# Compact retention output, a lag of three blocks and a new load order in a fused retention and feed-forward kernel

## The chip, the cores and the metric

The kernel runs on one core of one Trainium2 chip. The metric is device time in microseconds (us) of one execution. The kernel before was run again beside every experiment on the same chip. It took 249.6 to 253.2 us in all of these runs, mostly in two clusters near 249.8 and 252.5. The granted clock of PE was 1.00 over the runs of the lower one and 0.99 over those of the upper one; what starts the difference was not looked into. A ratio below is the mean time of one kernel's fast runs over the mean of the other's fast runs of the same rounds, so it is not quite the ratio of the medians quoted beside it.

Engine names in the profile: PE is the matmul engine (PEld its weight loads), DVE the vector engine, ACT the scalar engine, POOL the GpSimd engine, SPq the queue that issues most transfers. In the traces below each engine keeps the program order of its own instructions: PE stood for 6.05 us before one pair of score matmuls of the changed kernel while the matmuls behind them waited too.

## The reference

Retention for 4 batch rows, 8 heads, 768 steps and head size 64, followed by a feed-forward layer with 512 inputs and 2048 hidden units.

```python
def _attn_ref(q, k, v):
    gamma = 1.0 - 2.0 ** (-5.0 - np.arange(H))
    for t in range(S):
        state = gamma * state + einsum('bhd,bhe->bhde', k[:, :, t], v[:, :, t])
        y[:, :, t] = scale * einsum('bhd,bhde->bhe', q[:, :, t], state)

def _moe_ref(x, w_in, w_out):      # x: the 3072 tokens of y, heads side by side
    h = x @ w_in
    g = h * tanh(softplus(h))
    return g @ w_out
```

## The kernel before

The sequence is cut into 12 groups of 256 steps (two chunks of 128; three groups to a batch row). Heads go in pairs, so a group has four *units*. A unit has three steps:

```python
    def step_t(u):                       # T: transposes, then copies from PSUM
        ...
        for c in range(CG): nc.tensor.transpose(tp[:, 1, c], k16[:, c, hs(hp)], ident)
        for c in range(CG): nc.tensor.transpose(tp[:, 0, c], q16[:, c, hs(hp)], ident)
        nc.vector.tensor_copy(kt, tp[:, 1])
        nc.vector.tensor_copy(qp[0:64, :, 0], tp[0:64, 0])      # "pads": each head's q,
        nc.vector.tensor_copy(qp[64:128, :, 1], tp[64:128, 0])  # zeros for the other head

    def step_s(u):                       # S: scores, mask, state update
        for c in range(CG):
            nc.tensor.matmul(s_ps[:, c], kt[:, c], qp[:, c], start=True, stop=True)
        nc.vector.tensor_tensor(am, s_ps, msk[...], op=ALU.mult)
        ... # u_ps = k^T v per chunk; state = decay * state + u_ps, 128x128, on DVE

    def step_y(u):                       # Y: output, 256 columns = 2 heads x 128
        for c in range(CG):
            nc.tensor.matmul(y_ps[:, c], v16[:, c, hs(hp)], am[:, c], start=True, ...)
            if st is not None:
                nc.tensor.matmul(y_ps[:, c], st, qp[:, c], start=False, stop=True)
        for hh in range(2): nc.scalar.copy(xt[o:o + 64, ...], y_ps[o:o + 64, :, hh])
```

Half of what Y computes is thrown away: all 128 rows (two heads of v) meet all 256 columns (two heads of scores).

The retention steps are dealt out between the slices of the feed-forward layer. `f1` is one slice of the first matmul (8 matmuls of 256 columns), `f2` one of the second (4 of 512). Each block of 256 tokens has 8 slices, and f2 runs two blocks behind f1:

```python
    def att_ticks(u0, u1):
        for kk in range(u0, u1 + 2):
            yield lambda kk=kk: (step_y(kk - 2) ..., step_t(kk) ...)
            yield lambda kk=kk: (step_s(kk - 1) ...)
    ...
    for i in range(NG + 2):
        if i + 2 < NG: cast(i + 2)              # fp32 -> fp16, on GpSimd
        if i == 0:
            for j in range(NW): cast_wout(j)    # on GpSimd
        if 1 <= i and i + 3 < NG: load(i + 3)
        for a in range(NSL):
            ... # ticks up to i * NSL + a + 4
            if i < NG: f1(i, a)
            if 0 <= i - 2: f2(i - 2, a)
```

So a unit's T comes three ticks ahead of its S, and whole f1 slices lie in between. The loads are issued in the order group 0, four quarters of w_in, groups 1 and 2, four quarters of w_out, group 3, and so on.

## Time and profile before

| | before |
|---|---|
| median of its first 3 runs | 249.84 us |
| span of the profiled run | 250.4 us |
| PE busy | 220.4 us, 88% |
| first feed-forward matmul | 32.33 us |

The page of the kernel before, first part (busy us, share of the span, instructions) and second part (40 slices of the span, busy tenths; PEclk is the granted clock in tenths):

```profile
PE 220.4 (88%) x1696; PEld 157.5 (63%) x1696; DVE 116.5 (47%) x309; ACT 95.3 (38%) x195; POOL 85.1 (34%) x45
PE   0263199949999999999999999999999999999993
POOL 3102997679940450460640822703600000000000
DMA  8999999999912914916808609519210111011122
```

A slice is 6.26 us. PE is full from the sixth slice on, apart from one dip at 51 to 55 us. DMA is full for eleven slices: until about 67.5 us the kernel takes in data as fast as it can. From the dip on the kernel is bound by PE. The waits view of PE, the longest (line waited, releaser, us in total, times, longest):

```profile
PE tp L157 <- DVE k_142 L121: 9.2, 1, 9.2
PE tp L157 <- POOL k_277 L121: 7.8, 1, 7.8
PE tp L157 <- POOL k_504 L121: 3.7, 1, 3.7
```

These three waits are for the casts of groups 0, 1 and 3, and all three follow loads. In the timeline of PE, where idle time before a line would stand in brackets at its end, an early unit looks like this:

```profile
37.57 0.28 PE L157 MATMUL tp<-idtri,k_277 128*128 128x128 f16 x2
37.80 1.04 PE L228 MATMUL h_ps<-xt,win_87 128*128 128x256 f16 x8
38.67 0.38 PE L174 MATMUL s_ps<-qpad_90,kt 128*128 128x256 f16 x2
...
41.41 0.38 PE L174 MATMUL s_ps<-qpad_91,kt 128*128 128x256 f16 x2
```

The T at 37.57 has its S only at 41.41. Copies and pads have almost 4 us, and in these lines PE does not wait for them. One unit takes 2.74 us (38.67 to 41.41), and PE is full in it. Eight 256-column matmuls start 0.87 us apart in all.

### The profile page before, as it was taken

To read this page: it belongs to the slowest core of one execution; us is meant where nothing else is said; L and a number is where in the kernel's file an instruction comes from. 1 tells how busy PE (TensorE), PEld (TensorE's weight loads), DVE (VectorE), ACT (ScalarE), POOL (GpSimd) and SP (SyncE) were. 2 spreads that over 40 slices of the span, in tenths; PEclk is the share of its full clock that TensorE was granted. 3 is DMA by queue.
4 is the path that set the end of the run, shared out by engine and by line. 5 is a ranking of instruction groups with operands and counts; after the bars stand their busy time and mean duration, and the time that the engine had idled before them with its cause. 6 is when DMAs were issued, how large, how long until landed. Compare 5 with 4: busy or idle time off the path is not lost.

```text
span 250.4 us, 4251 instructions
## 1 busy us (share of the span) xinstructions
PE 220.4 (88%) x1696; PEld 157.5 (63%) x1696; DVE 116.5 (47%) x309; ACT 95.3 (38%) x195; POOL 85.1 (34%) x45
## 2 busy tenths in 40 slices
PE   0263199949999999999999999999999999999993
PEld 0141178827777777777777777777777777766441
DVE  1478567624455454535545553444655444101221
ACT  0324037624434445344444434444443444533000
POOL 3102997679940450460640822703600000000000
PEclk9999999998999999999999999999999999999999
DMA  8999999999912914916808609519210111011122
GB/s 162 297 387 263 218 287 387 256 207 227 181 42 66 225 46 106 195 40 149 190 0 176 162 3 229 106 46 228 66 42 0 45 45 41 3 42 45 44 81 84
DMA packets 82868, 33.91 MB, mean 135 GB/s; under 512 B 75552, under 2 KB 75680, under 8 KB 82848
## 3 DMA queue, kind: packets, MB, share of 16 engines
q1 hardware_dynamic: 82560, 33.56, 56.9%
q8 instruction: 13, 0.21, 0.4%
q10 hardware_dynamic: 288, 0.08, 0.1%
q14 instruction: 7, 0.06, 0.1%
HBM read 27.34 MB, written 6.29 MB: 134 GB/s over the span
## 4 chain that ended last, share of the span: by engine, by line
PE 77%; SPq 9%; DMA 7%; POOL 4%; issue 2%; DVE 0%; POOLq 0%
PE o_ps L241 33%; PE h_ps L228 29%; SPq L103 8%; DMA raw_q<-in_q_dram 4%; PE s_ps L174 3%; PE y_ps L205 3%; PE y_ps L209 3%; DMA raw_k<-in_k_dram 2%; PE tp L157 2%; PE tp L159 2%; PE u_ps L182 1%; SPq L130 1%; POOL q_276 L119 1%; POOL k_277 L121 1%; POOL k_504 L121 1%
## 5 line engine op out<-in xcount | busy, mean ns | idle before, releaser
L228 PE MATMUL h_ps<-xt,win_87 128*128 128x256 f16 x768 | 101.9, 277 | 0.0
L241 PE MATMUL o_ps<-wout_88,gt 128*128 128x512 f16 x384 | 95.9, 379 | 0.0
L232 ACT ACTIVATE gt<-h_ps 128x512 f16<-128x512 f32 x96 | 57.3, 597 | 96.0 <-PE h_ps L228 95.7
L228 PEld LDWEIGHTS <-win_87 128*128 128x128 f16 x768 | 72.7, 99 | 9.6
L241 PEld LDWEIGHTS <-gt 128*128 128x128 f16 x384 | 37.6, 98 | 28.2
L212 ACT CAST xt<-y_ps 64x256 f16<-64x256 f32 x96 | 35.1, 365 | 31.1 <-PE y_ps L209 30.5
L176 DVE TENSOR_TENSOR am<-s_ps,msk 128x512 f16<-128x512 f32 x48 | 33.0, 687 | 26.9 <-PE s_ps L174 26.8
L162 DVE COPY kt<-tp 128x256 f16<-128x256 f16 x48 | 14.0, 291 | 52.3 <-PE tp L159 52.3
L246 DVE COPY osb<-o_ps 128x512 f32<-128x512 f32 x24 | 16.6, 691 | 42.6 <-PE o_ps L241 42.6
L191 DVE SCALAR_TENSOR_TENSOR tstate<-tstate,tab,u_ps 128x128 f16<-128x128 f16 x64 | 21.9, 342 | 1.1
L174 PEld LDWEIGHTS <-kt 128*128 128x128 f16 x96 | 9.9, 105 | 8.7
L209 PEld LDWEIGHTS <-tstate 128*128 128x128 f16 x80 | 8.1, 101 | 4.1 <-DVE tstate L189 0.3
L157 PE MATMUL tp<-idtri,k_142 128*128 128x128 f16 x8 | 1.6, 308 | 10.1 <-DVE k_142 L121 9.2
L157 PE MATMUL tp<-idtri,k_277 128*128 128x128 f16 x8 | 1.3, 260 | 8.6 <-POOL k_277 L121 7.8
L142 POOL CAST wout_88<-wst 128x2048 f16<-128x2048 f32 x4 | 7.6, 1893 | 3.4 <-DMA wst<-in_moe_w_out_dram 3.2
L119 POOL TENSOR_TENSOR q_276<-raw_q,tab 128x1024 f16<-128x1024 f32 x1 | 2.8, 2777 | 16.1 <-DMA raw_q<-in_q_dram 16.1
L157 PEld LDWEIGHTS <-k_142 128*128 128x128 f16 x8 | 0.8, 126 | 10.6 <-DVE k_142 L121 9.2
L209 PE MATMUL y_ps<-qpad_91,tstate 128*128 128x256 f16 x28 | 7.4, 285 | 0.0
L209 PE MATMUL y_ps<-qpad_92,tstate 128*128 128x256 f16 x28 | 7.1, 278 | 0.0
L157 PEld LDWEIGHTS <-k_277 128*128 128x128 f16 x8 | 0.7, 110 | 9.5 <-POOL k_277 L121 8.2
L174 PE MATMUL s_ps<-qpad_91,kt 128*128 128x256 f16 x32 | 6.6, 291 | 0.0
L174 PE MATMUL s_ps<-qpad_92,kt 128*128 128x256 f16 x32 | 6.6, 291 | 0.0
(147 smaller groups left out, 226.9 us busy)
## 6 DMA issues: line engine op xcount, KB each, us to landing
raw_q<-in_q_dram SPq DMA_DIRECT2D x24, 256.0 KB, 5.0
raw_k<-in_k_dram SPq DMA_DIRECT2D x24, 256.0 KB, 5.1
raw_v<-in_v_dram SPq DMA_DIRECT2D x24, 256.0 KB, 5.0
out_dram<-osb SPq DMA_DIRECT2D x24, 256.0 KB, 2.0
wst<-in_moe_w_in_dram SPq DMA_DIRECT2D x4, 1024.0 KB, 9.2
wst<-in_moe_w_out_dram SPq DMA_DIRECT2D x4, 1024.0 KB, 10.4
idtri<-rn_identtri ACTq DMA_DIRECT2D x1, 64.0 KB, 3.1
tab<-rn_tab ACTq DMA_DIRECT2D x1, 10.0 KB, 1.9
```

The costliest lines, as they stand in the source:

```text
L103: nc.sync.dma_start(t[:, c], src[b, :, s0:s0 + C].rearrange("h p d -> p h d"))
L157: nc.tensor.transpose(tp[:, 1, c], k16[:, c, hs(hp)], ident)
L162: nc.vector.tensor_copy(kt, tp[:, 1])
L174: nc.tensor.matmul(s_ps[:, c], kt[:, c], qp[:, c], start=True, stop=True)
L176: nc.vector.tensor_tensor(am, s_ps, msk[:, hs(hp)].unsqueeze(1).broadcast_to((P, CG, 2, C)), op=ALU.mult)
L191: nc.vector.scalar_tensor_tensor(tn, states[-1], tab[:, 2 * H + hp:2 * H + hp + 1], u_ps[:, c], op0=ALU.mult, op1=ALU.add)
L209: nc.tensor.matmul(y_ps[:, c], st, qp[:, c], start=False, stop=True)
L212: nc.scalar.copy(xt[o:o + 64, hp, g * GT:(g + 1) * GT].rearrange("p (c i) -> p c i", i=C), y_ps[o:o + 64, :, hh])
L228: nc.tensor.matmul(h_ps[:, j], win16[:, bp, fb * P:(fb + 1) * P], xt[:, bp, i * GT:(i + 1) * GT], start=(bp == 0), stop=(bp == NBP - 1))
L232: nc.scalar.activation(gts[i][:, 2 * a:2 * a + 2], h_ps, AF.Mish, scale=inv_boost3)
L241: nc.tensor.matmul(o_ps, gts[i][:, fb, t * P:(t + 1) * P], wout16[:, fb], start=(fb == 0), stop=(fb == NFB - 1))
L246: nc.vector.tensor_copy(osb, o_ps)
```

## The change

The intent is to halve the wasted half of Y. The state matrix is kept block-diagonal, v is stored with a gap of zeros between the two heads, and both heads' outputs are accumulated into one 128-column tile. This takes 3 matmuls of 128 columns a chunk instead of 2 of 256, and one eviction instead of two. Along with it, feed-forward starts earlier through a new load order, f2 lags three blocks, and retention is put into fixed slots. The core of the diff (cut):

```diff
-        for c in range(CG):
-            nc.tensor.matmul(y_ps[:, c], v16[:, c, hs(hp)], am[:, c], ...)          # 256 columns
-            if st is not None:
-                nc.tensor.matmul(y_ps[:, c], st, qp[:, c], start=False, stop=True)  # 256 columns
+            if st is not None:
+                nc.tensor.matmul(y_ps[:, c], st, qt[:, c, hp], start=True, stop=False)   # 128
+            for hh in range(2):
+                nc.tensor.matmul(y_ps[:, c], vp[:, c * HP + hp, hh:hh + 2], am[:, c, hh], ...)  # 128
+        nc.scalar.copy(xts[g][:, hp], y_ps)
 ... state update
-            nc.vector.scalar_tensor_tensor(tn, states[-1], tab[...], u_ps[:, c], ...)  # 128x128
+            for hh in range(2):
+                o = slice(64 * hh, 64 * hh + 64)
+                nc.vector.scalar_tensor_tensor(tn[o, o], states[-1][o, o], ..., u_ps[o, c, o], ...)
 ... copies after the transposes
-        nc.vector.tensor_copy(qp[0:64, :, 0], tp[0:64, 0])
-        nc.vector.tensor_copy(qp[64:128, :, 1], tp[64:128, 0])
+        nc.vector.tensor_copy(qt[:, :, hp], tq[:, 0])
+        for hh in range(2):
+            nc.gpsimd.tensor_copy(qp[o:o + 64, :, hp, hh], qt[o:o + 64, :, hp])
 ... loads: group 0, w_in 0-1, group 1, w_in 2-3, groups 2 and 3, w_out
 ... schedule (slot = block * 8 + slice)
+    at(24, cast_wout, 0..3)                              # now on DVE
+    for g in range(4, NG):
+        s0 = max(20, (g - 1) * NSL - 12)
+        at(s0, cast, g, nc.gpsimd, nc.gpsimd, nc.gpsimd) # groups 4 and 5 both at slot 20
+    for g in range(1, NG):
+        for pos in range(-3, 7):                         # T at odd pos, S and Y at even pos
+            if g < 4: slot = (g - 1) * NSL + 4 + ((pos + 3) * 4) // 10   # half a block
+            else:     slot = (g - 1) * NSL + pos
+    for i in range(NG + LAG): ...                        # LAG = 3
```

The order of instructions shows two consequences. S now comes one slot after its T at most. In the first unit of groups 1 to 3 no matmul lies between the two. And GpSimd has the six casts of groups 4 and 5 ahead of the first pads of group 3.

More of the change, by code (lines that the diff above doesn't have):

```diff
@@ L42 @@
     FBW = NFB // NW
+    DT = 99
     BOOST = 16.0
-    inv_boost3 = float(1.0 / BOOST**3)
+    inv_boost = float(1.0 / BOOST**2)
     scale = float(1.0 / np.sqrt(D))
@@ L69 @@
     wst = ctx.enter_context(tc.tile_pool(name="rn_wst", bufs=4))
-    attp = ctx.enter_context(tc.tile_pool(name="rn_att", bufs=3))
-    stp = ctx.enter_context(tc.tile_pool(name="rn_state", bufs=3))
-    gtp = ctx.enter_context(tc.tile_pool(name="rn_gt", bufs=4))
-    outp = ctx.enter_context(tc.tile_pool(name="rn_out", bufs=3))
+    amp = ctx.enter_context(tc.tile_pool(name="rn_am", bufs=2))
+    xtp = ctx.enter_context(tc.tile_pool(name="rn_xt", bufs=3))
+    gtp = ctx.enter_context(tc.tile_pool(name="rn_gt", bufs=5))
+    outp = ctx.enter_context(tc.tile_pool(name="rn_out", bufs=2))
     psp = ctx.enter_context(
@@ L76 @@
     ctx.enter_context(tc.manual_schedule())
+    NPB = 3
     tab = cpool.tile([P, 2 * H + HP], FP32)
@@ L82 @@
     wout16 = cpool.tile([P, NFB, d_model], FP16)
-    xt = cpool.tile([P, HP, B * S], FP16)
-    NQP = 3
-    qpads = [
-        cpool.tile([P, CG, 2, C], FP16, name=f"qpad{i}") for i in range(NQP)]
+    qpads = [cpool.tile([P, CG, HP, 2, C], FP16, name=f"qpad{i}") for i in range(NPB)]
+    vpads = [cpool.tile([P, CG * HP, 3, D], FP16, name=f"vpad{i}") for i in range(NPB)]
+    sts = [[cpool.tile([P, P], FP16, name=f"st{h}_{i}") for i in range(3)]
+           for h in range(HP)]
     ident = idtri[:, 0:P]
@@ L106, in load, with cast @@
         raws[g] = got
-    def cast(g):
+    def cast(g, qe, ke, ve):
         q2, k2, v2 = raws.pop(g)
@@ L111, in cast @@
         k16 = castp.tile([P, CG, H, D], FP16, tag="k16", name="k16")
-        v16 = castp.tile([P, CG, H, D], FP16, tag="v16", name="v16")
-        first = g == 0
+        qt = castp.tile([P, CG, HP, C], FP16, tag="qt", name="qt")
+        kt = castp.tile([P, CG, HP, C], FP16, tag="kt", name="kt")
+        vp = vpads[g % NPB]
         def bc(lo):
@@ L117, in bc, with dma_transpose, pad @@
                 (P, CG, H, D))
-        nc.gpsimd.tensor_tensor(q16, q2, bc(0), op=ALU.mult)
-        ke = nc.vector if first else nc.gpsimd
+        qe.tensor_tensor(q16, q2, bc(0), op=ALU.mult)
         ke.tensor_tensor(k16, k2, bc(H), op=ALU.mult)
-        if first:
-            nc.scalar.mul(v16, v2, BOOST)
-        else:
-            nc.gpsimd.tensor_scalar(v16, v2, BOOST, None, op0=ALU.mult)
-        casted[g] = (q16, k16, v16)
+        src = v2.rearrange("p c (x y) d -> p (c x) y d", y=2)
+        if ve is nc.scalar:
+            ve.copy(vp[:, :, 0:3:2], src)
+        else:
+            ve.tensor_copy(vp[:, :, 0:3:2], src)
+        casted[g] = (q16, k16, vp, qt, kt, qpads[g % NPB])
+    def dma_transpose(g):
+        q16, k16, vp, qt, kt, qp = casted[g]
+        for dst, src in ((kt, k16), (qt, q16)):
+            nc.sync.dma_start_transpose(
+                dst.rearrange("p c x j -> p (c x) j"),
+                src.rearrange("p c h d -> p (c h d)"))
+    def pad(g):
+        q16, k16, vp, qt, kt, qp = casted[g]
+        for hh in range(2):
+            o = 64 * hh
+            nc.vector.tensor_copy(qp[o:o + 64, :, :, hh], qt[o:o + 64])
     def load_win(j):
@@ L141, in cast_wout @@
     def cast_wout(j):
-        nc.gpsimd.tensor_copy(
+        nc.vector.tensor_copy(
             wout16[:, j * FBW:(j + 1) * FBW], wraw.pop(("out", j)))
     state = [None] * HP
+    nst = [0] * HP
+    xts = {}
     live = {}
@@ L150, in hs, with step_t, step_s @@
         return slice(hp * 2, hp * 2 + 2)
-    def step_t(u):
-        g, hp = divmod(u, HP)
-        q16, k16, v16 = casted[g]
-        tp = psp.tile([P, 2, CG, C], FP16, tag="tp", name="tp")
+    def step_t(g, hp):
+        if g >= DT:
+            return
+        q16, k16, vp, qt, kt, qp = casted[g]
+        tk = psp.tile([P, 2, CG, C], FP16, tag="tp", name="tk")
+        tq = tk
+        if g == 0:
+            tq = psp.tile([P, 2, CG, C], FP16, tag="o_ps", name="tq", bufs=2)
         for c in range(CG):
-            nc.tensor.transpose(tp[:, 1, c], k16[:, c, hs(hp)], ident)
+            nc.tensor.transpose(tk[:, 1, c], k16[:, c, hs(hp)], ident)
         for c in range(CG):
-            nc.tensor.transpose(tp[:, 0, c], q16[:, c, hs(hp)], ident)
-        kt = attp.tile([P, CG, C], FP16, tag="kt", name="kt")
-        qp = qpads[u % NQP]
-        nc.vector.tensor_copy(kt, tp[:, 1])
-        nc.vector.tensor_copy(qp[0:64, :, 0], tp[0:64, 0])
-        nc.vector.tensor_copy(qp[64:128, :, 1], tp[64:128, 0])
-        live[u] = [kt, qp]
-    def step_s(u):
-        g, hp = divmod(u, HP)
+            nc.tensor.transpose(tq[:, 0, c], q16[:, c, hs(hp)], ident)
+        nc.vector.tensor_copy(kt[:, :, hp], tk[:, 1])
+        if g == 0:
+            nc.scalar.copy(qt[:, :, hp], tq[:, 0])
+        else:
+            nc.vector.tensor_copy(qt[:, :, hp], tq[:, 0])
+        for hh in range(2):
+            o = 64 * hh
+            nc.gpsimd.tensor_copy(qp[o:o + 64, :, hp, hh], qt[o:o + 64, :, hp])
+    def step_s(g, hp):
+        q16, k16, vp, qt, kt, qp = casted[g]
         cg = g % GPB
-        q16, k16, v16 = casted[g]
-        kt, qp = live[u]
         s_ps = psp.tile([P, CG, 2, C], FP32, tag="s_ps", name="s_ps")
         for c in range(CG):
-            nc.tensor.matmul(s_ps[:, c], kt[:, c], qp[:, c], start=True, stop=True)
-        am = attp.tile([P, CG, 2, C], FP16, tag="am", name="am")
+            nc.tensor.matmul(
+                s_ps[:, c], kt[:, c, hp], qp[:, c, hp], start=True, stop=True)
+        am = amp.tile([P, CG, 2, C], FP16, tag="am", name="am")
         nc.vector.tensor_tensor(
@@ L182, in step_s @@
             nc.tensor.matmul(
-                u_ps[:, c], k16[:, c, hs(hp)], v16[:, c, hs(hp)],
+                u_ps[:, c], k16[:, c, hs(hp)], vp[:, c * HP + hp, 0:3:2],
                 start=True, stop=True)
@@ L186, in step_s @@
         for c in range(nu):
-            tn = stp.tile([P, P], FP16, tag=f"st{hp}", name="tstate")
-            if states[-1] is None:
-                nc.vector.tensor_copy(tn, u_ps[:, c])
-            else:
-                nc.vector.scalar_tensor_tensor(
-                    tn, states[-1], tab[:, 2 * H + hp:2 * H + hp + 1], u_ps[:, c],
-                    op0=ALU.mult, op1=ALU.add)
+            tn = sts[hp][nst[hp] % 3]
+            nst[hp] += 1
+            for hh in range(2):
+                o = slice(64 * hh, 64 * hh + 64)
+                if states[-1] is None:
+                    nc.vector.tensor_copy(tn[o, o], u_ps[o, c, o])
+                else:
+                    nc.vector.scalar_tensor_tensor(
+                        tn[o, o], states[-1][o, o],
+                        tab[o, 2 * H + hp:2 * H + hp + 1], u_ps[o, c, o],
+                        op0=ALU.mult, op1=ALU.add)
@@ L194, in step_s, with step_y @@
             states.append(tn)
         state[hp] = states[-1]
-        live[u] += [am, states]
-    def step_y(u):
-        g, hp = divmod(u, HP)
-        v16 = casted[g][2]
-        kt, qp, am, states = live.pop(u)
-        y_ps = psp.tile([P, CG, 2, C], FP32, tag="y_ps", name="y_ps")
+        live[g, hp] = (am, states)
+    def step_y(g, hp):
+        q16, k16, vp, qt, kt, qp = casted[g]
+        am, states = live.pop((g, hp))
+        if hp == 0:
+            xts[g] = xtp.tile([P, HP, GT], FP16, tag="xt", name="xt")
+        y_ps = psp.tile([P, CG, C], FP32, tag="y_ps", name="y_ps")
@@ L203, in step_y @@
         for c in range(CG):
             st = states[c]
-            nc.tensor.matmul(
-                y_ps[:, c], v16[:, c, hs(hp)], am[:, c],
-                start=True, stop=st is None)
             if st is not None:
-                nc.tensor.matmul(y_ps[:, c], st, qp[:, c], start=False, stop=True)
-        for hh in range(2):
-            o = 64 * hh
-            nc.scalar.copy(
-                xt[o:o + 64, hp, g * GT:(g + 1) * GT].rearrange(
-                    "p (c i) -> p c i", i=C),
-                y_ps[o:o + 64, :, hh])
+                nc.tensor.matmul(
+                    y_ps[:, c], st, qt[:, c, hp], start=True, stop=False)
@@ L218 @@
+            for hh in range(2):
+                nc.tensor.matmul(
+                    y_ps[:, c], vp[:, c * HP + hp, hh:hh + 2], am[:, c, hh],
+                    start=(st is None and hh == 0), stop=(hh == 1))
+        nc.scalar.copy(xts[g][:, hp], y_ps)
     gts = {}
@@ L228, in f1 @@
                 nc.tensor.matmul(
-                    h_ps[:, j], win16[:, bp, fb * P:(fb + 1) * P],
-                    xt[:, bp, i * GT:(i + 1) * GT],
+                    h_ps[:, j], win16[:, bp, fb * P:(fb + 1) * P], xts[i][:, bp],
                     start=(bp == 0), stop=(bp == NBP - 1))
         nc.scalar.activation(
-            gts[i][:, 2 * a:2 * a + 2], h_ps, AF.Mish, scale=inv_boost3)
+            gts[i][:, 2 * a:2 * a + 2], h_ps, AF.Mish, scale=inv_boost)
     def f2(i, a):
@@ L253 @@
     load(0)
-    for j in range(NW):
-        load_win(j)
+    load_win(0)
+    load_win(1)
     load(1)
+    load_win(2)
+    load_win(3)
     load(2)
-    for qp in qpads:
-        nc.gpsimd.memset(qp, 0.0)
+    for i in range(NPB):
+        e = nc.vector if i == 0 else nc.gpsimd
+        if i == 0:
+            e.memset(vpads[i][:, :, 1], 0.0)
+            for h in range(HP):
+                for t in sts[h][:1]:
+                    nc.gpsimd.memset(t, 0.0)
+        else:
+            e.memset(vpads[i][:, :, 1], 0.0)
+        e.memset(qpads[i][0:64, :, :, 1], 0.0)
+        e.memset(qpads[i][64:128, :, :, 0], 0.0)
+    for h in range(HP):
+        for t in sts[h][1:]:
+            nc.gpsimd.memset(t, 0.0)
     for h in range(H):
@@ L262 @@
             msk[:, h], idtri[:, P:2 * P], float(gamma[h] ** (-C)), None, op0=ALU.mult)
-    cast(0)
+    cast(0, nc.vector, nc.vector, nc.scalar)
+    load(3)
     for j in range(NW):
         load_wout(j)
-    load(3)
-    def att_ticks(u0, u1):
-        for kk in range(u0, u1 + 2):
-            yield lambda kk=kk: (
-                step_y(kk - 2) if u0 <= kk - 2 < u1 else None,
-                step_t(kk) if kk < u1 else None)
-            yield lambda kk=kk: (
-                step_s(kk - 1) if u0 <= kk - 1 < u1 else None)
@@ L276 @@
-    for go in att_ticks(0, HP):
-        go()
-    for j in range(NW):
-        cast_win(j)
-    cast(1)
-    NSL = 8
-    rest = list(att_ticks(HP, NG * HP))
-    done = 0
-    for i in range(NG + 2):
-        if i + 2 < NG:
-            cast(i + 2)
-        if i == 0:
-            for j in range(NW):
-                cast_wout(j)
-        if 1 <= i and i + 3 < NG:
-            load(i + 3)
-        for a in range(NSL):
-            want = min(len(rest), i * NSL + a + 4)
-            if i + 1 >= NG:
-                want = len(rest)
-            while done < want:
-                rest[done]()
-                done += 1
+    NSL = 8
@@ new lines, with at @@
+    LAG = 3
+    slots = {}
+    def at(slot, fn, *args):
+        slots.setdefault(slot, []).append((fn, args))
+    for hp in range(HP + 2):
+        if 0 <= hp - 2:
+            step_y(0, hp - 2)
+        if hp < HP:
+            step_t(0, hp)
+        if 0 <= hp - 1 < HP:
+            step_s(0, hp - 1)
+    for j in range(2):
+        cast_win(j)
+    at(3, cast, 1, nc.gpsimd, nc.vector, nc.scalar)
+    at(3, load, 4)
+    at(3, cast_win, 2)
+    at(4, cast_win, 3)
+    at(8, cast, 2, nc.gpsimd, nc.vector, nc.scalar)
@@ new lines @@
+    at(8, load, 5)
+    at(16, cast, 3, nc.gpsimd, nc.vector, nc.scalar)
+    at(16, load, 6)
+    for j in range(NW):
+        at(24, cast_wout, j)
+    for g in range(4, NG):
+        s0 = max(20, (g - 1) * NSL - 12)
+        at(s0, cast, g, nc.gpsimd, nc.gpsimd, nc.gpsimd)
+        if g + 3 < NG:
+            at(s0, load, g + 3)
+        if g >= DT:
+            at(s0 + 4, dma_transpose, g)
+            at((g - 1) * NSL - 4, pad, g)
+    for g in range(1, NG):
+        for pos in range(-3, 7):
+            if g < 4:
+                slot = (g - 1) * NSL + 4 + ((pos + 3) * 4) // 10
+            else:
+                slot = (g - 1) * NSL + pos
+            if pos % 2 == 0:
+                if 0 <= pos // 2 < HP:
+                    at(slot, step_y, g, pos // 2)
+                if 0 <= pos // 2 + 1 < HP:
+                    at(slot, step_s, g, pos // 2 + 1)
+            elif 0 <= (pos + 3) // 2 < HP:
+                at(slot, step_t, g, (pos + 3) // 2)
@@ L300 @@
+    for i in range(NG + LAG):
+        for a in range(NSL):
+            for fn, args in slots.pop(i * NSL + a, []):
+                fn(*args)
             if i < NG:
                 f1(i, a)
-            if 0 <= i - 2:
-                f2(i - 2, a)
+            if 0 <= i - LAG:
+                f2(i - LAG, a)
+    assert not slots
 _INS = ['q', 'k', 'v', 'moe_w_in', 'moe_w_out']
```

## The prediction

> **What bounds the kernel now.** The page shows PE busy 88% of a 250.4 us span; the busy row by slices is at 9 from about 31 us on. Counting streamed columns (768x256 + 384x512 feed-forward, 104,448 retention) at the pitch of the timeline (eight 256-column matmuls start 0.87 us apart, two 128-column ones 0.11 us) gives some 207 us of PE work. The other 43 us lie at the start: PE waits until 9.25 us for the first cast, retention of block 0 runs as a latency chain to 21.5, PE idles to 29.3 for group 1, and again from 51 to 55 behind a GpSimd cast that waited for its load (chain of waits). Last matmul to end of span: 3 to 4 us. DMA is saturated until about 67.5 us (windows view: 218 GB/s for q/k/v, 387 for weights): by then groups 0 to 5 and both weights are in, and only then.
>
> **What the change does.**
> 1. Output matmuls stream 128 columns instead of 256 twice: 512 columns less a unit against 256 more, net 10,240 columns, 4.3 us of PE. Full-tile eviction halves ACT's copies (0.74 us to about 0.4); ACT is not critical.
> 2. DVE per unit stays near 2 us: two pad copies (0.27, 0.29) become one; two state updates (0.34) become four of 64x64, an estimated 0.25 each. The pads go to GpSimd, estimated 0.35 each, so each unit gains a DVE-to-GpSimd-to-PE hop.
> 3. Two w_in quarters come before group 1, so feed-forward starts near 24 us instead of 32.
> 4. Retention of blocks 1 to 3 is squeezed into half blocks with few matmuls between transposes, scores and outputs; I expect about 10 us per group where PE has 6.7 us of work.
> 5. The order of instructions shows GpSimd running the casts of groups 4 AND 5 before the pads of group 3. The last of them needs group 5's v, which lands no earlier than 67.5 us because the same 17.8 MB precede it. In-order PE stands at the first scores of group 3 meanwhile: it arrives near 58 and leaves near 69.6.
> 6. The four w_out casts (1.65 us each, estimated from the w_in casts) sit in DVE in one run of 6.6 us ahead of group 4's masks, just when the lagged second matmul starts.
>
> **Sum.** At the first scores of group 3, 65,024 columns (27.1 us) of 487,424 (203.1 us) are done. The head start is therefore lost in the stall, and so is the shorter PE stream: 69.6 + 176.0 + 3.8 (tail) = 249.4 us without any further loss. Losses: retention of group 3 paced by DVE, about 3; w_out casts and the scores behind them, about 5; clock after the stall, about 2 (in before, the window 55 to 60 us after a 3.7 us stall had a granted clock of 0.66; the Trainium skill, "TensorE: Matmul & The Clock Gate", section "What's actually happening", gives half clock after an idle window of about 3.4 us, and this trace agrees: eight matmuls took 1.71 us instead of 0.87); GpSimd cast bursts delaying pads later, about 3.
>
> Predicted: 263 us, 80% range 254 to 271. Faster by over 2%: 0.06; within 2%: 0.12; slower: 0.82.
>
> **What would show it.** PE idle for some 10 us up to about 69 us, released by a GpSimd pad copy behind the group 5 v cast that waited for DMA; feed-forward's first matmul near 24 us; a shorter gap near 82 to 92 us behind the w_out casts; DMA saturated to about 67 us as before; PE busy nearly full later.
>
> **What would make it wrong.** Group 5 landing clearly before 67 us, or PE late to slot 20 anyway (step 5 then costs less than it seems); the w_out casts hidden; steady blocks stalling on the GpSimd hop (slower still).

## More of the kernel before

All runs quoted here are of the undisturbed state.

The profiled run itself took 252.17 us, so it is of the upper cluster.

## The result, and the profile after

The changed kernel took 281.23 us (median of 4, 280.28 to 281.54), against 251.06 us (4 runs) for the kernel before. The ratio is 1.120, with a 95% interval from 1.111 to 1.129. It is slower, as predicted, but by 30 us instead of 13, outside the stated range. Its page, the same lines:

```profile
PE 227.1 (82%) x1792; PEld 160.7 (58%) x1792; DVE 130.6 (47%) x348; ACT 81.8 (29%) x154; POOL 91.2 (33%) x145
PE   0277747649175889998998999989899999999994
POOL 8231123139822318145172272541912211000000
PEclk9999997999868799999999999999999999999999
DMA  9999999989999005909339011101110111111222
```

PE starts earlier, but has no unbroken run of full slices before the sixteenth (a slice is 6.96 us here), and there is a hole in the eleventh. The granted clock dips in that slice and in the three after it, and before that in the seventh. Even later slices show 8s, where the kernel before had 9s throughout. The waits of PE on the pads now lead its list after the start (three buffers of one kind):

```profile
PE s_ps L198 <- POOL qpad_89 L191: 12.6, 6, 6.0
PE s_ps L198 <- POOL qpad_90 L191: 10.1, 8, 1.7
PE s_ps L198 <- POOL qpad_91 L191: 6.0, 6, 1.5
```

The three lines make 28.7 us. They understate the gaps, since each wait is counted after the modelled end of the matmul before it: at 36.11 below, the wait is 1.69 us, and the matmul before began 2 us earlier.

**One turn of an early unit.** The timeline of all engines from the scores of group 1's first unit to those of its second (start, duration, engine, line, what; idle before it in brackets; cut: the lines of PE that are not on this path, and those of PEld, ACT and SPq, are left out):

```profile
32.41 0.38 PE L198 MATMUL s_ps<-qpad_90,kt 128*128 128x256 f16 x2 [1.49 <-POOL qpad_90 L191]
32.74 0.28 PE L181 MATMUL tk<-idtri,k_348 128*128 128x128 f16 x2
32.83 0.69 DVE L201 TENSOR_TENSOR am<-s_ps,msk 128x512 f16<-128x512 f32 x1 [1.38 <-PE s_ps L198]
33.43 0.58 DVE L219 SCALAR_TENSOR_TENSOR st_2_97<-st_1_96,tab,u_ps 64x64 f16<-64x64 f16 x2
34.05 0.59 DVE L219 SCALAR_TENSOR_TENSOR st_0_95<-st_2_97,tab,u_ps 64x64 f16<-64x64 f16 x2
34.67 0.29 DVE L184 COPY kt<-tk 128x256 f16<-128x256 f16 x1
34.88 0.28 DVE L188 COPY qt<-tk 128x256 f16<-128x256 f16 x1
35.22 0.83 POOL L191 COPY qpad_90<-qt 64x256 f16<-64x256 f16 x2 [2.87 <-DVE qt L188]
36.11 0.38 PE L198 MATMUL s_ps<-qpad_90,kt 128*128 128x256 f16 x2 [1.69 <-POOL qpad_90 L191]
```

Nothing in this chain overlaps. The transposes of the next unit are done at 33.1, but their copies stand in DVE's queue behind this unit's mask and four state updates, the pads stand behind the copies, and the next scores behind the pads: 0.42 + 0.60 + 1.24 + 0.55 + 0.89 = 3.70 us from one S to the next (differences of the start times above). Group 1 repeats exactly this period: 32.41, 36.11, 39.81, 43.51.

**The hole.** GpSimd's timeline, from the cast of group 3's q (line 124 casts q, 125 k, 130 v; of groups 1 to 3 GpSimd casts only q) to the first pads of group 3, and the scores of PE that waited for these:

```profile
62.60 1.90 POOL L124 TENSOR_TENSOR q_734<-raw_q,tab 128x1024 f16<-128x1024 f32 x1
64.46 2.88 POOL L124 TENSOR_TENSOR q_791<-raw_q,tab 128x1024 f16<-128x1024 f32 x1
67.31 1.90 POOL L125 TENSOR_TENSOR k_792<-raw_k,tab 128x1024 f16<-128x1024 f32 x1
69.15 1.04 POOL L130 CAST vpad_93<-raw_v 128x1024 f16<-128x1024 f32 x1
70.15 1.90 POOL L124 TENSOR_TENSOR q_807<-raw_q,tab 128x1024 f16<-128x1024 f32 x1
72.01 1.90 POOL L125 TENSOR_TENSOR k_808<-raw_k,tab 128x1024 f16<-128x1024 f32 x1
73.85 1.04 POOL L130 CAST vpad_94<-raw_v 128x1024 f16<-128x1024 f32 x1
74.83 0.85 POOL L191 COPY qpad_89<-qt 64x256 f16<-64x256 f16 x2
75.73 0.59 PE L198 MATMUL s_ps<-qpad_89,kt 128*128 128x256 f16 x2 [6.05 <-POOL qpad_89 L191]
```

No line of GpSimd has a bracket: GpSimd worked without a pause for 13 us and waited for no load. PE did the transposes of group 3 at 69.30 and its scores only at 75.73.

**Where the time lies.** The windows view, core line by stretch (stretch, length, then busy time of PE, PEld, DVE, ACT and POOL with instruction counts, then granted clock, DMA share and GB/s), first of the kernel before:

```profile
24.50:70.00 45.50, 35.77 (x307) 28.69 (x308) 24.32 (x65) 18.45 (x40) 39.37 (x19) 0.96 1.10 245
70.00:100.00 30.00, 30.00 (x243) 21.87 (x241) 15.80 (x45) 13.38 (x28) 8.46 (x4) 1.00 0.45 100
100.00:230.00 130.00, 130.00 (x1027) 94.31 (x1026) 59.15 (x160) 55.69 (x115) 32.86 (x15) 1.00 0.39 89
```

and of the changed kernel:

```profile
24.50:70.00 45.50, 31.72 (x272) 25.55 (x272) 22.86 (x56) 16.99 (x32) 15.63 (x21) 0.96 1.06 263
70.00:100.00 30.00, 17.80 (x130) 13.30 (x131) 17.51 (x47) 5.35 (x12) 11.54 (x16) 0.77 0.81 147
100.00:230.00 130.00, 124.87 (x1073) 91.24 (x1072) 66.48 (x195) 44.85 (x86) 51.13 (x76) 1.00 0.28 66
```

The first feed-forward matmul came at 24.48 instead of 32.33 us, and yet PE was busy 4.1 us less by 70 us, 12.2 us less in the next 30 (where the clock was at 0.77 too), and 5.1 us less up to 230 us.

### The profile page after: what moved, and what is told of

Read it like the earlier page. It is cut to its first block, busy times and chain, and to the rows that moved or that the text cites. A ratio compares the mean times of both kernels' runs of the same rounds, so it can differ in the third digit from the quotient of the medians.

```text
span 278.5 us, 4570 instructions
## 1 busy us (share of the span) xinstructions
PE 227.1 (82%) x1792; PEld 160.7 (58%) x1792; DVE 130.6 (47%) x348; ACT 81.8 (29%) x154; POOL 91.2 (33%) x145
## 4 chain that ended last, share of the span: by engine, by line
PE 47%; POOL 16%; issue 15%; DVE 12%; DMA 6%; ACT 1%; SPq 1%; POOLq 0%; ACTq 0%
PE o_ps L267 20%; PE h_ps L255 17%; PE s_ps L198 4%; DMA raw_v<-in_v_dram 4%; DVE am L201 3%; DMA wst<-in_moe_w_out_dram 3%; POOL qpad_89 L191 3%; POOL qpad_91 L191 3%; POOL qpad_90 L191 2%; PE y_ps L239 2%; DVE wout_88 L160 2%; DVE kt L184 1%; SPq L107 1%; DVE qt L188 1%; PE tk L181 1%
## 5 line engine op out<-in xcount | busy, mean ns | idle before, releaser
L255 PE MATMUL h_ps<-xt,win_87 128*128 128x256 f16 x768 | 104.3, 284 | 2.1 <-DVE win_87 L152 1.4
L267 PE MATMUL o_ps<-wout_88,gt 128*128 128x512 f16 x384 | 94.6, 379 | 0.0
L255 PEld LDWEIGHTS <-win_87 128*128 128x128 f16 x768 | 75.1, 102 | 14.6 <-DVE win_87 L152 1.6
L191 POOL COPY qpad_90<-qt 64x256 f16<-64x256 f16 x32 | 14.6, 457 | 52.5 <-DVE qt L188 51.7
L191 POOL COPY qpad_91<-qt 64x256 f16<-64x256 f16 x32 | 12.7, 397 | 48.3 <-DVE qt L188 47.6
L242 ACT CAST xt<-y_ps 128x256 f16<-128x256 f32 x48 | 17.9, 372 | 33.9 <-PE y_ps L239 33.8
L184 DVE COPY kt<-tk 128x256 f16<-128x256 f16 x48 | 14.0, 292 | 25.2 <-PE tk L183 22.8
L191 POOL COPY qpad_89<-qt 64x256 f16<-64x256 f16 x32 | 12.7, 396 | 38.0 <-DVE qt L188 28.2
L198 PE MATMUL s_ps<-qpad_89,kt 128*128 128x256 f16 x32 | 7.5, 322 | 12.6 <-POOL qpad_89 L191 12.6
L198 PE MATMUL s_ps<-qpad_90,kt 128*128 128x256 f16 x32 | 6.5, 287 | 10.8 <-POOL qpad_90 L191 10.1
L188 DVE COPY qt<-tk 128x256 f16<-128x256 f16 x44 | 12.3, 280 | 0.0
L239 PE MATMUL y_ps<-am,vpad_92 128*128 128x128 f16 x64 | 9.3, 253 | 2.7 <-DVE am L201 2.7
L198 PE MATMUL s_ps<-qpad_91,kt 128*128 128x256 f16 x32 | 6.1, 271 | 6.0 <-POOL qpad_91 L191 6.0
L239 PEld LDWEIGHTS <-vpad_92 128*128 128x128 f16 x64 | 6.1, 111 | 6.0 <-DVE am L201 3.1
L181 PE MATMUL tk<-idtri,k_174 128*128 128x128 f16 x8 | 1.6, 304 | 9.4 <-DVE k_174 L125 9.3
L239 PE MATMUL y_ps<-am,vpad_93 128*128 128x128 f16 x64 | 7.8, 229 | 0.4 <-DVE am L201 0.4
L239 PE MATMUL y_ps<-am,vpad_94 128*128 128x128 f16 x64 | 7.5, 219 | 0.4 <-DVE am L201 0.4
```

The source lines that it names most:

```text
L184: nc.vector.tensor_copy(kt[:, :, hp], tk[:, 1])
L188: nc.vector.tensor_copy(qt[:, :, hp], tq[:, 0])
L191: nc.gpsimd.tensor_copy(qp[o:o + 64, :, hp, hh], qt[o:o + 64, :, hp])
L198: nc.tensor.matmul(s_ps[:, c], kt[:, c, hp], qp[:, c, hp], start=True, stop=True)
L239: nc.tensor.matmul(y_ps[:, c], vp[:, c * HP + hp, hh:hh + 2], am[:, c, hh], start=(st is None and hh == 0), stop=(hh == 1))
L242: nc.scalar.copy(xts[g][:, hp], y_ps)
```

## The experiments

Sixteen kernels ran beside the changed one, one of them a repetition of another. All but one gave correct outputs. The exception is named. *Before* is the median of the kernel before in the same rounds. The changed kernel itself ran in the first rounds only, so differences from it below are across rounds and chips, between which the median of the kernel before moved by 1.4 us.

| run | us | before | ratio |
|---|---|---|---|
| the changed kernel | 281.23 | 251.06 | 1.120 |
| changed, group 5's casts later | 279.20 | 252.45 | 1.111 |
| before + compact output | 253.59 | 252.45 | 1.009 |
| changed schedule, padded output | 262.20 | 252.45 | 1.043 |
| changed, lag of two | 279.88 | 252.45 | 1.112 |
| changed, pads by ACT | 260.13 | 251.85 | 1.035 |
| changed, transposes earlier | 263.08 | 251.85 | 1.047 |
| changed, both of these | 263.17 | 252.26 | 1.048 |
| changed, one state update (wrong) | 275.58 | 252.08 | 1.092 |
| before + load order | 259.76 | 251.85 | 1.032 |
| + compact output | 257.24 | 251.85 | 1.022 |
| + GpSimd's order mended | 246.85 | 252.26 | 0.981 |
| + feed-forward first | 244.59 | 252.26 | 0.972 |
| the same, padded output | 243.79 | 252.26 | 0.969 |
| the same again | 243.36 | 252.08 | 0.967 |
| the same, lag of three | 249.74 | 252.08 | 0.992 |
| hybrid output | 240.49 | 252.08 | 0.955 |

My theory after reading the trace (theory A) was that the order is at fault. Scores stand so close behind their transposes that DVE's copies and GpSimd's pads are laid bare, and GpSimd holds pads behind casts. The main rival (B) was that the compact output itself costs too much, through split state updates, many small matmuls and padded values.

### The casts of group 5 later

```diff
-        s0 = max(20, (g - 1) * NSL - 12)
+        s0 = 20 if g == 4 else max(24, (g - 1) * NSL - 12)
```

> The changed kernel (281 us), with only the casts of group 5 moved behind the pad copies of group 3 in GpSimd's order. Theory A (early retention is a serial chain through DVE and GpSimd, and GpSimd's own cast work, not the load, holds the first scores of group 3): the 6.05 us wait there shrinks by the 4.85 us that the three casts of group 5 took, time 274 to 277. Rival (DVE pacing would have held PE back anyway): less than 2 us gained, 279 to 281.

Measured: 279.20 us, in the rival's range. (The trace is of this kernel's slowest run, 281.15 us; the other four took 278.8 to 279.3.) The wait did shrink as computed, from 6.05 to 1.49 us, and group 3's first scores came at 71.58 instead of 75.73. The 24th slot began at 90.8 instead of 94.1. But the casts now stand among group 4's pads, where scores at 100.61 waited 2.09 us for them. The kernel gained 2 us net. Theory A had the wait right and the gain wrong: here, moving work within GpSimd's queue moved part of the wait along with it.

### The parts apart: compact output without the schedule, schedule without compact output

The first kernel is the one before with block-diagonal states, spaced values and 128-column outputs. Its pads stay on DVE, and ACT copies the unpadded q ahead of them. The second is the changed kernel with the old `step_t`, state update and `step_y` put back (both cut).

```diff
 # first                                         # second
-    y_ps[:, c], v16[:, c, hs(hp)], am[:, c]     -    nc.gpsimd.tensor_copy(qp[...], qt[...])
+    y_ps[:, c], st, qt[:, c]                    +    nc.vector.tensor_copy(qp[0:64, :, 0], tp[0:64, 0])
+    y_ps[:, c], vp[..., hh:hh + 2], am[:, c, hh]  +  y_ps[:, c], vp[:, c, hs(hp)], am[:, c]
```

> The kernel before, with the compact output alone (block-diagonal states, values padded between heads, 128-column output matmuls, one eviction; pads still by DVE, the unpadded q by ACT). Theory A: the compact output is not the cause; the PE stream is 10,240 columns (4.3 us) shorter and every wait stays, so 245 to 248 against 250 to 252 of before. Rival B (the compact output's split states and padded operands are the cause): well over before, 265 or more.

Measured: 253.59 us, 1.009 (1.002 to 1.017). Rival B is out as the main cause, but my gain was missing too. The trace shows that feed-forward began at 37.97 us instead of 32.33. The extra copy of q held the transposes up (the second unit's began at 13.69 us instead of 10.74), and the w_in casts took 8.9 us together instead of 6.3. In the first two blocks a unit took 3.26 us instead of 2.74. DVE was the limit, with its split updates and with 0.49 us in each unit in which its pads waited for ACT's copy of q, so this run charges the compact output with more than its own work. The shorter PE stream paid for part of that later. This run left open whether the compact output gains anything; the last pair of runs answers that.

> The changed kernel's load order, schedule and lag of three, with the old padded output and the old DVE pads. Theory A: the schedule alone already loses, since it puts scores one slot or none behind their transposes, but a unit of the chain without the GpSimd hop and with two state updates takes about 2.5 us instead of 3.7: 255 to 263. Rival B (compact output is the cause): 250 or less. Rival C (schedule is everything): near 281.

Measured: 262.20 us, inside theory A's range. A unit of group 1 took 2.51 us (30.38, 32.88, 35.39), nearly as computed. So the schedule loses some 10 us without any compact output, the compact output about 1 us without the schedule, and both together 30 us. They are not additive. But the hop to GpSimd is present only where both are, so part of what they do together is the hop.

### A lag of two blocks in the changed kernel

```diff
-    LAG = 3
+    LAG = 2
-        at(24, cast_wout, j)
+        at(16, cast_wout, j)
```

> The changed kernel with a lag of two blocks and the w_out casts one block earlier. Theory A: blocks 2 and 3 have PE idle in the chain, and the second matmuls of block 0 (32 of 512 columns, 6.9 us) can fill part of it: 274 to 278. Rival: the lag only moves work, 280 to 282.

Measured: 279.88 us, between the two. PE's waits on the pads fell from 28.7 to 23.9 us, and 1.8 us of waits for the w_out casts came in. The extra work fills little while S stands behind T in PE's own order: what comes later in the queue did not fill a gap in front of it.

### Pads by ACT; transposes earlier; both

```diff
 # pads by ACT, put ahead of DVE's two copies
-            nc.gpsimd.tensor_copy(qp[o:o + 64, :, hp, hh], qt[o:o + 64, :, hp])
+            nc.scalar.copy(qp[o:o + 64, :, hp, hh], tq[o:o + 64, 0])
 # transposes two positions earlier, no operation changed
-        for pos in range(-3, 7):
-            if g < 4: slot = (g - 1) * NSL + 4 + ((pos + 3) * 4) // 10
-            elif 0 <= (pos + 3) // 2 < HP: at(slot, step_t, g, (pos + 3) // 2)
+        for pos in range(-5, 7):
+            if g < 4: slot = (g - 1) * NSL + 3 + ((pos + 5) * 5) // 12
+            elif 0 <= (pos + 5) // 2 < HP: at(max(slot, 21) if g == 4 else slot, step_t, ...)
```

> The changed kernel with the two pad copies of a unit done by ACT straight from PSUM, ahead of DVE's two copies, instead of by GpSimd behind them. Theory A (the DVE-to-GpSimd hop sits in a serial chain of 3.7 us a unit, and pads queue behind GpSimd's casts): a unit of groups 1 to 3 takes about 2.8 us, the 6 us stall before group 3's scores and the later waits on GpSimd pads (27 us of PE waits in all) go: 255 to 262. Rival (the two extra state updates on DVE are the cost, not the hop): 274 or more.

Measured: 260.13 us, inside theory A's range. The scores of group 1 came every 2.62 us (31.68, 34.30, 36.93, 39.55). Two copies moved from one little-used engine to another saved 21 us. The edit did two things, though: it took away the hop, and it put the pads ahead of DVE's copies. This run does not part the two.

> The changed kernel with every transpose from group 1 on two positions earlier, so that copies and pads of a unit are done while the unit before is scored; no operation changes. Theory A (the loss is the order: pads exposed between transpose and scores): a unit of groups 1 to 3 falls from 3.7 us to DVE's own 2.3 to 2.6 us, the later waits on pads vanish, part of the stall behind the casts of groups 4 and 5 stays: 254 to 264. Rival (amount of work on DVE and GpSimd, not the order): 274 or more.

Measured: 263.08 us, inside theory A's range. Here not one operation differs from the changed kernel, only the order (in groups 1 to 3 the scores of the third unit and the outputs of the second also moved one slot earlier), and 18 us went. The period in group 1 is 2.36 us. Group 3's scores still waited 8.61 us behind the casts, until 72.39. GpSimd came earlier to these casts in this run (60.43 us instead of 64.46), and now the loads of group 5 did hold it, for 1.5 us in all:

```profile
65.98 1.90 POOL L124 TENSOR_TENSOR q<-raw_q,tab 128x1024 f16<-128x1024 f32 x1 [0.81 <-DMA raw_q<-in_q_dram]
68.25 1.90 POOL L125 TENSOR_TENSOR k<-raw_k,tab 128x1024 f16<-128x1024 f32 x1 [0.37 <-DMA raw_k<-in_k_dram]
70.51 1.04 POOL L130 CAST vpad<-raw_v 128x1024 f16<-128x1024 f32 x1 [0.36 <-DMA raw_v<-in_v_dram]
```

This is the wait for the load of group 5 that the prediction had put at 67.5 us and after. It is there, but in the changed kernel GpSimd was later still.

> The changed kernel with both repairs, pads by ACT from PSUM and transposes two positions earlier. Theory A: the two overlap (each takes the pads off the chain) but leave different waits: 248 to 256, below either alone (260 and 263). Rival (they remove the same wait): 258 to 262.

Measured: 263.17 us, a miss; the rival's number came nearer, for a reason that neither theory had. The new first line in the waits of PE is

```profile
PE tk L181 <- DVE qt L191: 9.4, 9, 2.7
```

All transposes of a group go through one PSUM tile, so the next T waits until DVE has emptied the tile, and DVE's copies stand behind the state updates. With early transposes the same DVE queue is waited for at another place. A second tile for the transposes was not tried.

### One state update instead of two

```diff
-            for hh in range(2):
-                o = slice(64 * hh, 64 * hh + 64)
+            for o in [slice(0, P)]:
```

> The changed kernel with one 128x128 state update instead of two of 64x64; wrong on purpose, since the states then hold cross terms between the two heads. Theory A: the two updates are in the serial chain of a unit, 3.7 us falls to about 3.1 us in group 1 and less in groups 2 and 3 with one chunk's update or fresh states, 4 to 7 us in all: 274 to 277. Rival (the hop to GpSimd alone matters): 279 to 281.

Measured: 275.58 us, outputs wrong. The period in group 1 fell from 3.70 to 3.09 us (31.47, 34.56, 37.65). So the split updates are some 6 of the 30 us. They are there because they stand in the chain; DVE as a whole is busy 47% of the span.

### The load order by itself

```diff
     load(0)
-    for j in range(NW): load_win(j)
-    load(1); load(2)
-    ...
-    for j in range(NW): load_wout(j)
-    load(3)
+    load_win(0); load_win(1); load(1); load_win(2); load_win(3); load(2)
+    ...
+    load(3)
+    for j in range(NW): load_wout(j)
```

> The kernel before, with the new load order alone (two w_in quarters, group 1, two quarters, groups 2 and 3, then w_out; the last two quarters cast two slots later; k and v of group 1 cast by DVE and ACT). Theory A (the load order is sound by itself): feed-forward starts about 4 us earlier and the 3.7 us wait for group 3's load goes: 241 to 246. Rival (later w_out, or casts on DVE, give it back): 249 to 253.

Measured: 259.76 us, a clear miss. Feed-forward began at 27.3 us, as hoped, but PE then waited 11.65 us for group 3's k. GpSimd still had the four w_out casts ahead of it in its queue, and w_out now lands later:

```profile
47.63 1.89 POOL L142 CAST wout<-wst 128x2048 f16<-128x2048 f32 x1 [7.91 <-DMA wst<-in_moe_w_out_dram]
...
59.57 1.90 POOL L121 TENSOR_TENSOR k<-raw_k,tab 128x1024 f16<-128x1024 f32 x1
```

Group 3 itself had been loaded before w_out. A new load order needs the same order in the queue that consumes the loads.

> As the run with the load order alone, plus the compact output (pads by DVE from PSUM as before, unpadded q by ACT last, zeroing by GpSimd). Theory A: the 4.3 us shorter PE stream counts where PE is full (from the third block on), DVE's two extra state updates cost some of it back in the first two blocks: 2 us below to equal with the load order alone, 239 to 246. Rival (compact output costs more than it saves): 3 us or more above it.

Measured: 257.24 us, with the same 11.1 us wait in it: 2.5 us below the load order alone, slightly more than theory A had; its range in us fell with the run that it builds on.

```diff
-        if i + 2 < NG: cast(i + 2)
         if i == 0:
+            cast(2); cast(3)
             for j in range(NW): cast_wout(j)
+        elif 2 <= i and i + 2 < NG: cast(i + 2)
```

> As the run with load order and compact output on the kernel before, with GpSimd's casts of group 3 put ahead of its four w_out casts. Theory A (an in-order GpSimd holding a cast that waits for its load ahead of work that is ready): the 11.1 us wait of PE for group 3's k goes, w_out casts delay the first second-layer matmuls by 2 to 4 us instead, 243 to 249. Rival (the load order is bad as such, since w_out comes later): 254 or more.

Measured: 246.85 us. Group 3's three casts went ahead of the four w_out casts, and 10.4 us went. This is the first version that beats both kernels (0.981 of the kernel before, 0.975 to 0.988).

```diff
-    for j in range(2): cast_win(j)
-    cast(1)
+    cast_win(0); cast(1); cast_win(1)
...
+            if i == 0 and a == 0: want = 0      # first f1 slice ahead of group 1's transposes
```

> As the run with GpSimd's order mended, and the first feed-forward slice ahead of group 1's transposes, with only the first w_in quarter cast before group 1's k. Feed-forward starts near 22 to 23 us instead of 28: 1 to 4 us below that run, 240 to 246. If the start is given back by later waits for loads: equal to it within 1 us.

Measured: 244.59 us, with feed-forward from 25.27 us on, later than I expected.

### What the compact output is worth

> The same schedule as the run with feed-forward first, with the old padded output. Theory A (compact output saves 4.3 us of PE stream wherever PE is full, and costs only DVE time in the first blocks): 1 to 4 us above it. Rival (compact output is worth nothing or less): equal or below it.

Measured: 243.79 us, 0.8 us below the compact one: the rival's side, by less than the two runs can settle. The traces show both halves of the balance. With the compact output feed-forward starts at 25.27 us, with the padded one at 22.52. In group 2 a unit takes 2.92 us against 2.72, and PE waits for DVE's split updates there (0.17 us in each unit, after the modelled end of the matmul before). Later the compact one makes up for most of this. So the two were joined. Groups 0 to 2 keep the padded output, and from group 3 on, where a new batch row starts its states afresh, the output is compact (`if g < 3:` in each step).

> The mended schedule, with the padded output for groups 0 to 2 and the compact one from group 3 on (where a new batch row starts its states afresh). Theory A (the compact output saves its columns only where PE is full and costs DVE time where it is not): 9 of 12 groups save 3.2 us of PE stream and the first blocks lose nothing, 239.5 to 241.5, some 3 us below the padded run. Rival (128-column matmuls or the extra evictions cost PE as much as they save): equal to the padded run within 1 us.

> The padded run of the mended schedule once more, on the same chip as the hybrid, for a difference of about 1%: 243 to 245.

Measured, in the same five rounds: hybrid 240.49 us (0.955, 0.950 to 0.960), padded 243.36 us (0.967, 0.963 to 0.972). The difference is 2.9 us, against 3.2 us computed from the columns of nine groups. The runs scatter by about as much as that (239.8 to 242.3 and 242.9 to 244.4), but do not overlap. Within this scatter the compact output is worth what its columns say where PE is full. The hybrid is the fastest version found: 11.6 us below the kernel before in the same rounds and 41 us below the changed kernel. The longest waits of its PE, after the one for the first cast, are short; those of the first line all lie before 29 us. (The trace is of its slowest run, 242.27 us.)

```profile
PE y_ps L229 <- DVE am L192: 3.5, 4, 1.0
PE tp L168 <- POOL k L132: 1.8, 2, 1.5
```

### A lag of three blocks in a schedule without the other waits

```diff
-    for i in range(NG + 2): ... f2(i - 2, a)
+    for i in range(NG + 3): ... f2(i - 3, a)      # and a fifth buffer for g (cut)
```

> The padded run of the mended schedule with a lag of three blocks instead of two. Theory A (the lag only moves work, and costs where the third block is short of PE work): 0 to 3 us above the padded run. Rival (a lag of three spares PE the waits for w_out): 1 to 4 us below it.

Measured: 249.74 us, 6.4 us above the padded run and more than I expected. Without second-layer matmuls in the third block PE reaches group 4's transposes at about 58 us, sooner than loads and casts allow. It waits 4.0 us there for group 4's k, whose GpSimd cast began at 60.38, and starts again at half clock. In the padded run, second-layer matmuls fill PE from 52.47 us on, and the same cast (begun at 60.82) costs 0.24 us. The longer lag takes away the work that hid it.

## Why the prediction was right or wrong

The direction and most places of the waits were right. The sizes, and one of the causes, were not. Two of the things that the prediction named as able to make it wrong came true: PE late to slot 20, and steady blocks that stall on the pads.

- **Step 1, the shorter stream (right).** 4.3 us were predicted for twelve groups. The hybrid shows 2.9 us for nine.
- **Step 2, DVE and pads per unit (too small).** Half-size updates were put at 0.25 us each, and measured 0.31 from one to the next; pads at 0.35, measured 0.40 to 0.41 (0.83 for a unit's two).
- **Step 3, the start (right).** 24 us predicted, 24.48 measured.
- **Step 4, "about 10 us per group" (the step that failed).** The three groups took far longer: in group 1 the time from the first transposes to the last outputs is 15.9 us (30.54 to 46.4), in group 2 it is 12.9 (51.53 to 64.4), in group 3, with the hole in it, 22.6 (69.30 to 91.9). I had added up DVE's work, about 2 us a unit, and taken the rest as overlapping. It does not overlap. Every link waits for the one before, the links of two units meet in DVE's queue, and the period is their sum, 3.70 us. Pads by ACT (2.62 us), one update (3.09) and early transposes (2.36) each take out or move one link and show that period. PE came to group 3's transposes at 69.3 us, not at 58; groups 1 and 2 make 8.8 of these 11 us.
- **Step 5, the hole (right place, wrong cause).** GpSimd did run the casts of groups 4 and 5 first. But as PE and GpSimd were late by then, it was GpSimd's own 10 us of casts that ended last, and not the load. The stall was 6 us, not 10, and PE left it at 75.7 us, not at 69.6. The run with early transposes shows the load wait that I had in mind.
- **Step 6, the w_out casts (small).** They took 5.0 us instead of 6.6, and the scores behind them waited 1.2 us. In their place the units of group 3, at 3.6 to 4.3 us each, filled the time to 92 us.
- **The sum.** From group 3's first scores to the 24th slot I counted about 12 us, work and losses. It took 18.4 (75.7 to 94.1), in which the windows view gives a granted clock of 0.69. The half clock after a stall was in the prediction at 2 us for one stall. In this trace PE fell back to it three times, from 43.51, 75.73 and 88.51 us on (granted clock 0.62, 0.61 and 0.50 in the windows 43.5 to 47.9, 75.7 to 82.4 and 88.5 to 94.5). Only the second came after a wait longer than the 3.7 us of the kernel before. The first followed a wait of 1.69 us, the third two of 1.69 and 0.67 us; equal waits at 36.11 and 39.81 us had no such effect, but before the first PE had waited for 4.0 of the last 5.4 us. What decides was not tested. After the 24th slot began, 405,248 columns were left, 168.9 us at 2.4 columns per ns, and PE needed 180.3 us: the waits on GpSimd and DVE listed after 94 us make about 6 us. A part of the rest is that the sums took N/2.4 ns for a matmul of N columns (the prediction's 207 us are that, though it names the pitch of the timeline, which gives some 212). The Trainium skill, "TensorE: Matmul & The Clock Gate", section "Back-to-back issue gap", adds about 2.5 ns at full clock in its formula for a single matmul. This trace roughly agrees (eight matmuls of 256 columns in 0.87 us, 108.8 ns each, against 106.7), and over the 1,376 matmuls left that is an estimated 3.4 us with the skill's 2.5 ns. The remaining 2 us or so were not traced.

So the floor of 249.4 us left out the late arrival and the 2.5 ns, and the prediction put about 13 us on top of it where the kernel took 32 us more than it (281.2 - 249.4, the late arrival included). Some things stay open. The hop to GpSimd was not tried in the old schedule, the half clock was not taken out by itself, and the experiments inside the changed schedule (21, 18, 6 and 2 us) overlap, so they can't be added up.

## What to carry to other kernels

When a loop has a chain through several in-order engines, write down the time of one turn of the chain as a sum, and give each link the place in its engine's queue that it really has. Busy shares (DVE 47%, GpSimd 33% here) say nothing about it. Put the producers far enough ahead that the consumer never waits, as the kernel before did with three ticks between transposes and scores, and order the consuming queue as the loads are ordered. A saving in an engine's stream is worth its full size only where that engine is full; elsewhere use whichever variant is light on the engine that is the limit there.

## What the Trainium skill lacked or had wrong

- "TensorE: Matmul & The Clock Gate", section "Back-to-back issue gap", gives about 81 ns a matmul of 128 columns and about 131 ns of 512 for a real stream of weight loads and matmuls. Here each matmul has its own weight load, and pairs of 128 columns start 0.11 us apart (about 55 ns each) and four of 512 take 0.86 to 0.87 us (216 ns each). That is what the section gives for an isolated matmul, N/2.4 + 2.5 ns, at both sizes.
- "SBUF — State Buffer", section "Who interferes with whom", says that DVE copies and casts in two-port modes lock GpSimd out, and the times of this trace agree (the mode itself is not in the trace): two pad copies that take 0.83 us took 2.79 us while DVE ran the w_out casts. The same section says that a DVE operation with two SBUF inputs contends with GpSimd's reads. The q cast of 1.90 us took 2.88 us when DVE's k cast ran beside it. The sizes that it mentions ("GpSimd 1.5× slower") name no operations; these are 3.4 and 1.5 times.
- No page that I used has the figure for two small GpSimd copies in a dependency chain: 0.40 and 0.41 us for 64x256 fp16, and 0.89 us from the first start to the matmul that needs both.
